# Short tail tiles of a routed expert layer in slots of their own, with float32 products side by side on half the array's columns

## Chip, cores and metric

One core of one Trainium2 chip. The metric is the device time of one execution in microseconds (us), the median over several runs. An array engine (TensorE, "PE") multiplies; VectorE ("DVE"), ScalarE ("ACT") and GpSimd ("POOL") work on tiles; SyncE ("SP") issues most transfers.

## What is computed

Three layers follow one another: a clustered attention (batch 2, 8 heads, 768 positions, head width 64), a gated feed-forward layer, and an expert layer that sends each of 1536 tokens to one of 8 experts. The last is what the change touches:

```python
h = x @ w_in
x = (h * sigmoid(h)) @ w_out                   # (1536, 512) -> (1536, 2048) -> (1536, 512)
logits = x @ w_gate + modality_bias[modality_id]
e_idx = argmax(logits, axis=1)                 # one expert for each token
gate = softmax(logits)[e_idx]
for e in range(8):
    m = e_idx == e
    out[m] = gate[m] * (relu(x[m] @ w1[e]) @ w2[e])     # 512 -> 1024 -> 512
```

For the inputs that are timed the experts get 1, 1, 91, 688, 300, 455, 0 and 0 tokens. All data are float32.

## The kernel before

The kernel goes through attention (about 0 to 260 us of the span), the gated layer (to about 540) and the expert layer. The order of the instructions on every engine is fixed when the program is built: each step is given to a list scheduler by `op(engine, estimated ns, function, deps, uses, alloc, prio)`, with the buffers that it uses, and the scheduler writes one static order per engine. In the code below, numbers in `prio`, `xfer` and after `op("PE", ...` are such planning values.

**Routing.** As the rows of the gated layer's output are finished, they are written to DRAM together with their 8 logits (`x2d`), and DVE works out the expert of each token and its rank within the expert. When the last logits are there, `count()` (L1173) counts the tokens, and from them the number of 128-row tiles of each expert (`nt`, by comparing the counts with 0, 128, 256 and so on) and the first tile of each expert (`cux`). `tiles()` (L1182) makes a one-hot table `bt` from each token's tile; twelve products of `bt` with a matrix of token numbers (L1189) give, for each tile (column) and row (partition), the token's number: `idin`, with a large offset `padb` for rows that stand empty. It also works out each tile's expert (`eti`) and whether that differs from the tile before. The first two tiles belong to the first expert and are known earlier. Experts are taken in a cyclic order that begins with the first full one, here expert 3.

**Tiles.** `slot()` (L1319) is one tile: 128 rows of one expert. `NBASE` = 16 such tiles are always in the program; a conditional block (`rest()`, L1455) holds the others up to 21 and runs only if there are more. The sixteen here are 6, 3, 4, 1, 1 and 1 tiles of the six experts, so that the expert changes in front of tiles 6, 9, 13, 14 and 15 (counted from 0). A tile does this:

- weights: 8 chunks of 512 KB (four of `w1`, four of `w2`), loaded on SP's queue (L1312, L1315) only if the expert has changed, each into one buffer of its own (`w4`), which the tile before must have read;
- split: float32 products in full tiles are made as three products of a shorter format (fp32r): high by high, high by low, low by high. So every tile splits each chunk again, high part by ACT (L202), low part by DVE (L200), into one of ten `whl` buffers;
- gather: POOL fetches the 128 rows by their numbers (L1355); four transposes on PE (L1360) and a split (ACT L1364, DVE L1367) make `xb`;
- first layer (L1381): 8 steps of three products, 128 rows by 512 columns, the sum of 512 inputs in four chunks; ACT takes the positive part (L1396); eight transposes (L1401) and a split (ACT L1406, DVE L1409);
- second layer (L1423): 8 steps of three products; ACT scales by the gate (L1446), POOL scatters the rows to the output (L1449). The scatter's row numbers lie in a small buffer `gt`, of which there are two; DVE writes them (L1435) when the scatter that used the buffer before has landed.

Of the kernel before, what the change touches and what calls it, by code (L numbers as in the profile page):

```python
# [176 lines left out]
F32 = mybir.dt.float32  # L177
F32R = mybir.dt.float32r
# [9 lines left out]
P = 128  # L188
# [570 lines left out]

NT, DM, DF, F2, NE = 1536, 512, 2048, 1024, 8  # L760
NTC = NT // P
NBASE = 16
NFIRST = 2
NSLOT = NTC + NE + 1
XR = DM + NE
X8 = 768

# [4 lines left out]
def moe(tc, sc, pools, att, xT, w_in, w_out, mod_id, w_gate, mod_bias, w1, w2, out, ident, tails, opts):  # L772

    nc = tc.nc
    if True:
# [14 lines left out]
        def op(eng, dur, fn, prio=0.0, **kw):  # L790
            return sc.op(eng, dur, fn, prio=prio + 1000.0, **kw)
# [17 lines left out]
        def main():  # L809
            if a_ops:  # L810
                pools.close("a_ps", "a_sb", "a_cst")
            pools.open("m_sb", reuse_waits="tile")
            pools.open("m_ps", space=PSUM, reuse_waits="tile")
            late.update(Am=pools["m_sb"].tile([P, NTC, P], F16, name="Am"), bt=pools["m_sb"].tile([P, NTC, NSLOT], F16, name="bt"))
# [13 lines left out]
        io1 = small("io1", [P, NSLOT])  # L828
        thr = small("thr", [P, NTC])
        ebg = small("ebg", [P, NE], BF16)  # L830
        wg = small("wg", [P, 4, NE])
        mids = small("mids", [P, 2, NC6, 2], I32)
# [4 lines left out]
        def consts():  # L837
            g = nc.gpsimd
            kw = dict(allow_small_or_imprecise_dtypes=True)
            g.iota(io128, [[1, P]], base=0, channel_multiplier=0, **kw)  # L840
            g.iota(iop, [[0, 1]], base=0, channel_multiplier=1, **kw)
            g.iota(ids, [[S, 2], [1, NC6]], base=1, channel_multiplier=NC6, **kw)
            g.iota(io8, [[1, NE]], base=0, channel_multiplier=0, **kw)
            g.iota(tie8, [[-1, NE]], base=NE, channel_multiplier=0, **kw)
            g.iota(io1, [[1, NSLOT]], base=0, channel_multiplier=0, **kw)
            g.iota(thr, [[P, NTC]], base=0, channel_multiplier=0, **kw)
            g.memset(ones, 1.0)
            g.memset(ebg, 0.0)

        def consts2():  # L850
            V.tensor_scalar(tri, io128, iop[:, 0:1], None, ALU.is_gt)
        o_c = op("Pool", 1800, consts, prio=0)
        o_c2 = op("DVE", 300, consts2, deps=[o_c], prio=50)

# [169 lines left out]
        cmp_, xn = small("cmp_", [P, NE, NTC]), small("xn", [P, NE, NE])  # L1024
        ntot, ntoti = small("ntot", [P, 1]), small("ntoti", [P, 1], I32)
        tt, et = [small(n, [P, NSLOT]) for n in ("tt", "et")]
        dd = small("dd", [P, NSLOT, NE])
        e0i, eti = small("e0i", [P, 1], I32), small("eti", [P, 2, NSLOT], I32)
        idin, padb = small("idin", [P, NSLOT], U32), small("padb", [P, NSLOT])
# [4 lines left out]
        def chain(eng, prio, deps, steps, lat=None, dur=80, uses=()):  # L1034

            o = None
            for n, f in enumerate(steps):
                f, d = f if isinstance(f, tuple) else (f, dur)
                o = op(eng, d, f, deps=(deps if o is None else [o]), uses=uses if n == 0 else (), prio=prio, lat=lat)
            return o  # L1040
# [130 lines left out]
                lambda: V.tensor_scalar(padb[:, :NFIRST], ib.tile[:, :NFIRST], 0.0, 4096.0, ALU.is_equal, ALU.mult)], uses=[ib])  # L1171

        def count(o, lb, pr):  # L1173
            stat["nt"] = chain("DVE", pr + 5, [o, stat["e0"]], [
                lambda: V.tensor_tensor(cnt, lb.tile[:, 2 * NE:3 * NE], gapv, ALU.add),
                lambda: V.tensor_tensor(cmp_, cnt.unsqueeze(2).to_broadcast([P, NE, NTC]),
                                        thr.unsqueeze(1).to_broadcast([P, NE, NTC]), ALU.is_gt),
                lambda: V.tensor_reduce(nt, cmp_, AX.X, ALU.add),
                lambda: V.tensor_tensor(xn, before, nt.unsqueeze(1).to_broadcast([P, NE, NE]), ALU.mult),
                lambda: V.tensor_reduce(cux, xn, AX.X, ALU.add)], uses=[lb])  # L1180

        def tiles(pr):  # L1182

            ib = Buf("bank")

            def f():
                ib.tile = pst(ib)
                for j in range(NTC):
                    nc.tensor.matmul(ib.tile[:, :NSLOT], late["Am"][:, j], late["bt"][:, j], start=(j == 0), stop=(j == NTC - 1))  # L1189
            b12 = lambda v: v.unsqueeze(1).to_broadcast([P, NTC, NE])  # L1190
            o = chain("DVE", pr + 5, [stat["nt"]] + [stat["r", j] for j in range(NTC)], [
                (lambda: V.tensor_tensor(pm, ohb, b12(cux), ALU.mult), 165),
                (lambda: V.tensor_reduce(rk, pm, AX.X, ALU.add), 165),
                lambda: V.tensor_tensor(rk, rk, rkf[:, 0], ALU.add),
                (lambda: V.tensor_tensor(late["bt"], io1.unsqueeze(1).to_broadcast([P, NTC, NSLOT]),
                                         rk.unsqueeze(2).to_broadcast([P, NTC, NSLOT]), ALU.is_equal), 320)])
            o = op("PE", 400, f, deps=[o] + [stat["A", j] for j in range(NTC)], uses=[ib], alloc=[ib], prio=pr)
            stat["i", 1] = chain("DVE", pr + 5, [o], [
                lambda: V.tensor_scalar(idin[:, NFIRST:], ib.tile[:, NFIRST:NSLOT], -1.0, 0.0, ALU.add, ALU.max),
                lambda: V.tensor_scalar(padb[:, NFIRST:], ib.tile[:, NFIRST:NSLOT], 0.0, 4096.0, ALU.is_equal, ALU.mult)], uses=[ib])  # L1200

            stat["e"] = chain("DVE", pr + 5.5, [stat["nt"]], [
                lambda: V.tensor_tensor(cue, cux, nt, ALU.add),
                lambda: V.tensor_reduce(ntot, nt, AX.X, ALU.add),
                lambda: V.tensor_scalar(tt, io1, 1.0, ntot[:, 0:1], ALU.add, ALU.min),
                (lambda: V.tensor_tensor(dd, be(tt), bt8(cue), ALU.is_gt), 230),
                (lambda: V.tensor_reduce(et, dd, AX.X, ALU.add), 230),
                lambda: V.tensor_tensor(eti[:, 1, 1:], et[:, 1:], et[:, :-1], ALU.not_equal),
                lambda: V.tensor_scalar(tt, et, est[:, 0:1], float(NE), ALU.add, ALU.is_ge),
                lambda: V.scalar_tensor_tensor(et, tt, -float(NE), et, ALU.mult, ALU.add),  # L1210
                lambda: V.tensor_scalar(eti[:, 0], et, est[:, 0:1], None, ALU.add),
                lambda: V.tensor_copy(ntoti, ntot)])  # L1212

        cp = dict(w1=-55.8, w2=-29.9, ws=4.5, m1=-25.6, m2=1.6, tx=-46.9, rl=-24.5, ga=-47.5, g0=15, g4=15, gx=14, hi='AAAAAAAA', lo='DDDDDDDD', xyh='DDAAAADD', xyl='DDDDDDDD')
        cp.update(opts.get("C", {}))
        EN = {"A": "Act", "D": "DVE", "P": "Pool"}
        for b in range(2):
# [19 lines left out]
            for fc in range(16):  # L1237
# [4 lines left out]
                for x in range(2):  # L1242
# [76 lines left out]
        def slot(op, t):  # L1319
# [130 lines left out]
                                             bounds_check=NT - 1, oob_is_err=False)  # L1450
            o = op("Act", 570, fo, deps=[o, oe], uses=[ob, os_, eb], alloc=[os_], prio=pr)
            op("Pool", 1040, fs, deps=[o], uses=[os_, eb], prio=pr + 20, xfer=728, name=f"scatter{t}")
        for t in range(NBASE):
            slot(op, t)
        def rest():  # L1455
# [74 lines left out]
```

## Time and profile before

| what | value |
|---|---|
| median of 3 runs (lowest to highest) | 761.03 us (760.16 to 762.56) |
| the profiled execution | 761.42 us |
| its span, granted clock of PE | 759.3 us, 0.989 |
| busy: PE, DVE, ACT, POOL | 736.2, 574.7, 519.4, 272.0 us |
| bytes moved by DMA | 93.27 MB |

The span runs from the first to the last recorded instruction. A row of the timeline merges neighbouring instructions of one line: its start, its length, the engine, the line of the kernel, what is written and read, the shapes and the number of instructions; at the end, in brackets, how long the engine had stood idle and what ended that. The instructions overlap in the pipeline, so that the time one costs is read from the start of it to the start of the next. PE's clock has two levels here, 2.4 GHz (1.00) and 1.2 GHz.

### The profile page before, as it was taken

Reading aid. Unit: us, or ns where it says so; the run is one execution under the profiler, and the core shown is the slowest. Engines: PE = TensorE matmul, PEld = TensorE weight load, DVE = VectorE, ACT = ScalarE, POOL = GpSimd, SP = SyncE. Lnnn points to the kernel's source line nnn. Section 1 sums busy time; section 2 is a strip of 40 time slices with the busy share of each in tenths; the row PEclk is TensorE's granted clock in tenths of the full one; section 3 lists DMA queues with packets and bytes.
Section 4 is the critical chain, followed back from the end, with each engine's and each line's share of the span. In section 5 each row is a group of like instructions: output and inputs, shape, how many; then the busy total and the mean of one; then the engine's idle time right before and its main releaser. Section 6 shows DMA issues by size and latency. Waiting matters only on the chain. (4 is left out here: it accounts for less than half of the span.)

```text
span 759.3 us, 12533 instructions
## 1 busy us (share of the span) xinstructions
PE 736.2 (97%) x4286; PEld 644.4 (85%) x4286; DVE 574.7 (76%) x1034; ACT 519.4 (68%) x951; POOL 272.0 (36%) x304
## 2 busy tenths in 40 slices
PE   8999998999999899999999999999999999999995
PEld 7889887999989799999988989998778887888774
DVE  7978898889889698888477444423978869788972
ACT  7989987998998655554344343323659887898772
POOL 6887765887764100000004000000322424434441
PEclk9999999999999999999999999999999999999998
DMA  8852643522240067665206711000211443515961
GB/s 207 187 131 65 161 116 84 129 70 67 73 133 1 22 236 247 246 234 182 85 16 212 294 63 56 28 0 1 85 30 57 145 161 105 165 51 164 336 212 56
DMA packets 58197, 93.27 MB, mean 123 GB/s; under 512 B 27086, under 2 KB 31950, under 8 KB 58128
## 3 DMA queue, kind: packets, MB, share of 16 engines
q1 hardware_dynamic: 55568, 85.00, 37.0%
q0 software_dynamic: 2560, 7.41, 3.1%
q8 instruction: 36, 0.59, 0.3%
q14 instruction: 33, 0.27, 0.1%
HBM read 101.85 MB, written 15.78 MB: 155 GB/s over the span
## 5 line engine op out<-in xcount | busy, mean ns | idle before, releaser
L200 DVE TENSOR_TENSOR whl<-w,whl 128x1024 fp32r<-128x1024 f32 (+2 forms) x132 | 149.4, 1175 | 2.8 <-ACT whl L202 2.6
L1255 PE MATMUL bank<-whl,whl 128*128 128x384 f32 x768 | 146.9, 340 | 1.8 <-DVE whl L205 1.2
L1255 PEld LDWEIGHTS bank<-whl,whl 128*128 128x128 f32 x768 | 136.8, 190 | 7.7 <-DVE whl L205 1.6
L202 ACT ACTIVATE whl<-w 128x1024 fp32r<-128x1024 f32 (+2 forms) x128 | 128.3, 1038 | 13.6 <-DMA w<-in_moe_w_dram 10.3
L1087 POOL TENSOR_SCALAR row<-L,mx 128x8 f32<-128x8 f32 x12 | 4.7, 394 | 271.1 <-DVE mx L1106 146.6
L1381 PE MATMUL bank<-whl,xb 128*128 128x512 f32 x384 | 97.8, 402 | 2.8 <-DVE whl L200 2.3
L602 DVE TENSOR_REDUCE nm<-big 128x1 f32<-128x768 f32 x96 | 91.0, 951 | 12.0 <-PE big L583 10.7
L1423 PE MATMUL bank<-whl,w 128*128 128x512 f32 x384 | 97.7, 401 | 0.0
L608 ACT ACTIVATE p<-big,nm 128x768 f32<-128x768 f32 x96 | 87.7, 914 | 4.0 <-DVE nm L602 3.7
L1381 PEld LDWEIGHTS bank<-whl,xb 128*128 128x128 f32 x384 | 70.4, 189 | 19.2 <-DVE whl L200 3.4
L1423 PEld LDWEIGHTS bank<-whl,w 128*128 128x128 f32 x384 | 71.3, 190 | 15.0
L622 PE MATMUL t<-ident,p 128*128 128x128 f32 x576 | 81.2, 276 | 2.7 <-ACT yb L714 2.0
L622 PEld LDWEIGHTS t<-ident,p 128*128 128x128 f32 x576 | 67.3, 141 | 12.2 <-issue 2.9
L1449 POOL DMA_INDIRECT out_dram<-row,gt_0i x8 | 29.3, 3661 | 65.6 <-ACT row L1446 50.6
L200 DVE TENSOR_TENSOR whl<-wraw,whl 128x1024 fp32r<-128x1024 f32 x31 | 37.9, 1224 | 15.7 <-ACT whl L202 15.7
L202 ACT ACTIVATE whl<-wraw 128x1024 fp32r<-128x1024 f32 x31 | 32.7, 1057 | 20.5 <-DVE wraw L955 16.3
L656 DVE TENSOR_TENSOR pt_1l<-t,pt_1h 128x384 fp32r<-128x384 f32 x66 | 34.9, 553 | 13.4 <-ACT pt_1h L202 12.6
L1355 POOL DMA_INDIRECT row<-x2d,idin x16 | 34.6, 2165 | 12.9 <-DVE ntoti L1212 5.0
L1270 ACT ACTIVATE g_0s<-bank 128x384 f32<-128x384 f32 x16 | 7.9, 492 | 42.7 <-PE bank L1255 42.7
L700 PE MATMUL t<-pt_0h,vn 128*128 128x384 f32 x96 | 35.1, 366 | 1.0 <-POOL yb L200 0.5
L580 PE MATMUL big<-opn_1K,opn_1QQ 128*128 128x384 f32 x96 | 34.7, 361 | 1.1 <-ACT p L608 1.1
L580 PE MATMUL big<-opn_0K,opn_0QQ 128*128 128x384 f32 x96 | 34.5, 364 | 0.8 <-ACT p L608 0.6
(294 smaller groups left out, 1648.8 us busy)
## 6 DMA issues: line engine op xcount, KB each, us to landing
w<-in_moe_w_dram SPq DMA_DIRECT2D x120, 512.0 KB
w<-in_moe_w_out_dram SPq DMA_DIRECT2D x8, 1024.0 KB
wraw<-wsc SPq DMA_DIRECT2D x16, 512.0 KB
wsc<-wraw SPq DMA_DIRECT2D x15, 512.0 KB
w<-in_moe_w_in_dram SPq DMA_DIRECT2D x7, 1024.0 KB
x2d<-row SPq DMA_DIRECT2D x12, 260.0 KB
rawv<-in_v_dram SPq DMA_DIRECT2D x8, 384.0 KB
rawq<-in_q_dram SPq DMA_DIRECT2D x14, 192.0 KB
```

Source lines behind the costliest of these rows:

```text
L200: (nc.vector if e == "DVE" else nc.gpsimd).tensor_tensor(dst, a, b, op)
L202: nc.scalar.activation(dst, a, AF.Copy, scale=1.0 if scale is None else scale)
L580: nc.tensor.matmul(sb.tile[:, x, :HALF], t["QQ"][:, h, cs], t["K1"][:, h, sl(x)], start=True, stop=False)
L602: nc.vector.tensor_reduce(nb.tile, sb.tile[:, :, :HALF], AX.XY, ALU.max, negate=True)
L608: nc.scalar.activation(pb.tile.rearrange("p (a b) -> p a b", a=2), sb.tile[:, :, :HALF], AF.Exp, bias=nb.tile[:, 0:1], scale=1.0, accum_ou ...
L622: nc.tensor.transpose(tbs[x].tile[:, j * P:(j + 1) * P], pb.tile[:, kc * P:(kc + 1) * P], ident)
L656: nc.vector.tensor_tensor(hs(grp["tile"][1], x), src, hs(grp["tile"][0], x).bitcast(F32), ALU.subtract)
L700: nc.tensor.matmul(yb.tile[:, :HALF], o["vb"].tile[:, h, kc, :], grp["tile"][s][:, kc, :], start=(kc == 0 and s == 0), stop=(kc == NC6 - 1 ...
L1255: nc.tensor.matmul(hb.tile[:, :HALF], w[:, ws, dc, fs], xx[:, s, cs], start=(dc == 0 and n == 0), stop=(dc == 3 and n == 2))
L1355: nc.gpsimd.indirect_dma_start(gb.tile, None, x2d[:, :] if t >= NFIRST else x2d[:S], bass.IndirectOffsetOnAxis(idin[:, t:t + 1], 0))
L1381: nc.tensor.matmul(hbs[x].tile, xs_[:, s, dc], w.tile[:, ws, x * 512:(x + 1) * 512], start=(dc == 0 and n == 0), stop=(dc == 3 and n == 2))
L1423: nc.tensor.matmul(ob.tile, hT.tile[:, s, fc * P:(fc + 1) * P], w.tile[:, ws, i * 512:(i + 1) * 512], start=(fc == 0 and n == 0), stop=(fc ...
```

## The change

The last tile of an expert no longer has to be a full one. `count()` compares the counts with a second row of thresholds as well (64, 192, 320 and so on): an expert whose last tile holds 64 tokens or fewer is marked (`sm`), the first four of these in order get a small slot (`six` is its number), and their last tile is taken out of `nt`. `tiles()` moves the tokens of such tails to one of four further columns of the table, and twelve further products (L1257 after the change) give the small slots' row numbers. `NBASE` falls to 12. The counts here give 5, 2, 4 and 1 full tiles and four small slots with 48, 44, 1 and 1 tokens, so that the expert of full tiles changes three times, in front of tiles 5, 7 and 11, and each small slot loads its expert's 8 chunks without condition.

`small_slot()` puts both halves of the array's columns to use: its up to 64 tokens are the 64 stationary columns of two float32 products, which write to the two halves of the partitions of one bank of the accumulator. In the first layer (L1560) each half makes 512 of the 1024 hidden values, in the second (L1588) 256 of the 512 outputs. Nothing is split. Six of its chunks take the `g` buffers of the gated layer (four of them, so that the last two chunks follow in buffers that first products have read) and two a `wt` buffer. For that the `g` buffers' two halves become one tile, and the row buffers fall from 9 to 7. Slots stand at the full tiles 3, 6, 8 and 10.

```diff
-NBASE = 16
+NBASE = 12
+NSM = 4
+SMALL_AT = (3, 6, 8, 10)
...
+NCOL = NSLOT + NSM
...
-        TAGS = {"wraw": 3, "w64": 2, "wt": 1, "whl": 10, "row": 9, "xb": 2, "g": 4, "bank": 8, "w4": 8, "gt": 2, "lgt": 2}
+        TAGS = {"wraw": 3, "w64": 2, "wt": 1, "whl": 10, "row": 7, "xb": 2, "g": 4, "bank": 8, "w4": 8, "gt": 2, "lgt": 2}
...
+                (lambda: V.tensor_tensor(cmp_, bn(cnt, NTC), thr2.unsqueeze(1).to_broadcast([P, NE, NTC]), ALU.is_gt), 165),
+                (lambda: V.tensor_reduce(nf, cmp_, AX.X, ALU.add), 165),
+                lambda: V.tensor_tensor(sm, nt, nf, ALU.subtract),
+                lambda: V.tensor_tensor(xn, before, b8(sm), ALU.mult),
+                lambda: V.tensor_reduce(six, xn, AX.X, ALU.add),
+                lambda: V.scalar_tensor_tensor(sm, six, float(NSM), sm, ALU.is_lt, ALU.mult),
+                lambda: V.tensor_tensor(nt, nt, sm, ALU.subtract),
...
+                (lambda: V.tensor_tensor(pm, ohb, b12(nt), ALU.mult), 165),
+                (lambda: V.tensor_reduce(rkn, pm, AX.X, ALU.add), 165),
...
+                lambda: V.tensor_tensor(rkn, rkf[:, 0], rkn, ALU.is_ge),
...
+                lambda: V.scalar_tensor_tensor(rk, rkn, float(NCOL), rk, ALU.mult, ALU.add),
...
+        def small_slot(s):
...
+                loads.append(op("SP", 475, f, deps=[ov] + loads[-1:], uses=[rb], alloc=[] if c == 5 else [rb], prio=pr + cs["w"] + c, xfer=1456, name="wl"))
...
+                nc.gpsimd.indirect_dma_start(gb.tile, None, x2d[:, :], bass.IndirectOffsetOnAxis(idin[:, col:col + 1], 0))
...
+                    for x in range(2):
+                        nc.tensor.matmul(hb.tile[H[x]], xb.tile[:, dc * P + 64 * x:dc * P + 64 * x + 64], wt_(dc)[:, 512 * x:512 * x + 512],
+                                         start=(dc == 0), stop=(dc == 3))
...
+                        for y in range(2):
+                            nc.tensor.matmul(ob.tile[H[y], :256], hT.tile[:, j * P + 64 * x:j * P + 64 * x + 64], w[:, 256 * y:256 * y + 256],
+                                             start=(fc == 0), stop=(fc == 7))
...
+                nc.gpsimd.indirect_dma_start(out.rearrange("n (y c) -> (n y) c", y=2), bass.IndirectOffsetOnAxis(idsc[:, s:s + 1], 0), os_.tile, None,
+                                             bounds_check=2 * NT - 1, oob_is_err=False)
```

How the order of instructions moves, at three places. First PE around the products that make the row numbers (L1189 before, L1210 after), in the first two full tiles. Before, they follow the first layer of tile 1 (L1381):

```order
L1381 MATMUL bank_6611<-whl_6369,xb_6537 128x512 x3
L1381 MATMUL bank_6624<-whl_6369,xb_6537 128x512 x3
L1381 MATMUL bank_6611<-whl_6384,xb_6537 128x512 x3
L1381 MATMUL bank_6624<-whl_6384,xb_6537 128x512 x3
L1189 LDWEIGHTS Am
L1189 MATMUL bank_6697<-bt,Am 128x21
```

After, four steps of tile 0's second layer (L1477) and the eight transposes of tile 1's hidden values (L1455) have been drawn in front of them:

```order
L1435 MATMUL bank_6564<-whl_6335,xb_6458 128x512 x3
L1435 MATMUL bank_6575<-whl_6335,xb_6458 128x512 x3
L1477 MATMUL bank_6645<-whl_6355,w_1_6601 128x512 x6
L1455 MATMUL bank_6664<-ident,wraw_6650 128x128 x4
L1455 MATMUL bank_6671<-ident,wraw_6650 128x128 x4
L1477 MATMUL bank_6645<-whl_6371,w_1_6601 128x512 x6
L1210 LDWEIGHTS Am
L1210 MATMUL bank_6698<-bt,Am 128x21
```

Second, PE at the end of the last full tile after the change: the small products (L1560 first layer, L1588 second, `g` and `wt` the buffers of their chunks) of slots 2 and 3 stand between the steps of the second layer of tiles 10 and 11 (L1477). Here the order shows the last first-layer products of slot 3 and the later second-layer products of slot 2, where before there were only full steps:

```order
L1560 MATMUL bank_8398<-g_1w,xb_8258 64x512 x2
L1560 MATMUL bank_8398<-g_3w,xb_8258 64x512 x2
L1560 MATMUL bank_8398<-g_0w,xb_8258 64x512 x2
L1560 MATMUL bank_8398<-g_2w,xb_8258 64x512 x2
L1477 MATMUL bank_8421<-whl_8306,w_1_8401 128x512 x6
L1588 MATMUL bank_8309<-g_1w,w_0_8298 64x256 x4
L1571 MATMUL bank_8443<-ident,wraw_8425 128x128 x4
L1477 MATMUL bank_8421<-whl_8366,w_1_8401 128x512 x6
L1477 MATMUL bank_8421<-whl_8383,w_1_8401 128x512 x3
L1588 MATMUL bank_8309<-g_0w,w_0_8298 64x256 x4
L1477 MATMUL bank_8421<-whl_8383,w_1_8401 128x512 x3
L1477 MATMUL bank_8421<-whl_8392,w_1_8401 128x512 x3
```

So the chunk in `g_1w`, loaded anew after the first of these rows has read the buffer, is used again five rows later, and the one in `g_0w` seven rows after its own. Third, the last entries of SP's queue after the change (L1369 loads a chunk of `w2`; the rows of the address computation between them are left in):

```order
L1369 DMA wt_0a<-in_moe_w_dram 128x2x512
L1369 ISA
L1369 DMA wt_0x<-in_moe_w_dram 128x2x512
L1369 ISA
L1369 DMA g_1w<-in_moe_w_dram 128x2x512
L1369 ISA
L1369 DMA g_3w<-in_moe_w_dram 128x2x512
L1369 ISA
L1369 DMA g_0w<-in_moe_w_dram 128x2x512
L1369 ISA
L1369 DMA g_2w<-in_moe_w_dram 128x2x512
L1620 COMPARE_AND_BRANCH
```

The last two chunks of slots 2 and 3 are the four loads at its end, behind everything else; before, the queue ended with chunks of full tiles.

## Rows read from the trace of the kernel before

**Rows 1.** Busy time, share of the span and instructions of each engine, from the page.
```profile
PE 736.2 (97%) x4286; PEld 644.4 (85%) x4286; DVE 574.7 (76%) x1034; ACT 519.4 (68%) x951; POOL 272.0 (36%) x304
```

**Rows 2.** Stages: stretch, length; busy PE, PEld, DVE, ACT, POOL; clock; DMA share, GB/s.
```profile
626.40:642.50 16.10, 14.30 (x61) 11.19 (x60) 16.10 (x20) 12.15 (x18) 7.23 (x2) 0.89 0.32 95
642.50:655.00 12.50, 12.50 (x62) 10.24 (x61) 9.34 (x13) 11.67 (x17) 4.43 (x2) 1.00 0.36 121
704.60:718.60 14.00, 12.93 (x62) 10.15 (x61) 13.41 (x17) 10.57 (x16) 7.17 (x2) 1.00 0.98 338
```

**Rows 3.** Timeline of PE, tile 8: start, duration, line, operation, count; then idle before.
```profile
642.54 1.55 PE L1381 MATMUL bank<-whl,xb 128*128 128x512 f32 x6
643.94 0.60 PE L1360 MATMUL bank<-ident,row 128*128 128x128 f32 x4
644.29 4.44 PE L1381 MATMUL bank<-whl,xb 128*128 128x512 f32 x18
654.98 1.56 PE L1381 MATMUL bank<-whl,xb 128*128 128x512 f32 x6
```

**Rows 4.** Timeline of PE, last stage: where it waited.
```profile
633.28 2.02 PE L1381 MATMUL bank<-whl,xb 128*128 128x512 f32 x5 [1.80 <-DVE whl L200]
635.09 2.56 PE L1423 MATMUL bank<-whl,w 128*128 128x512 f32 x6
713.26 1.33 PE L1401 MATMUL bank<-ident,wraw 128*128 128x128 f32 x8 [1.05 <-ACT whl L202]
732.30 4.18 PE L1381 MATMUL bank<-whl,xb 128*128 128x512 f32 x17 [0.53 <-DVE xb L1367]
736.96 1.43 PE L1381 MATMUL bank<-whl,xb 128*128 128x512 f32 x5 [0.48 <-DVE whl L200]
```

**Rows 5.** Timeline of DVE at tile 6.
```profile
624.34 0.16 DVE L1435 TENSOR_TENSOR gt_0i<-idin,padb 128x1 uint32<-128x1 uint32 x1 [5.42 <-DMA out_dram<-row,gt_0i]
```

**Rows 6.** Timeline of PE in attention: pairs of 64 columns.
```profile
61.42 0.33 PE L583 MATMUL big<-opn_1KX,opn_1QX 96*128 96x384 f32 x1
61.68 0.32 PE L722 MATMUL t<-ident,sums_1r 128*64 128x128 f32 x1
61.69 0.32 PE L722 MATMUL t<-ident,sums_3r 128*64 128x128 f32 x1
61.84 0.27 PE L722 MATMUL t<-ident,sums_1r 128*64 128x128 f32 x1
62.29 0.27 PE L722 MATMUL t<-ident,sums_3r 128*64 128x128 f32 x1
62.49 0.66 PE L622 MATMUL t<-ident,p 128*128 128x128 f32 x4
```

**Rows 7.** Timeline of PE in attention: products on 32 columns, four abreast.
```profile
50.56 0.85 PE L444 MATMUL t<-full,cT 128*32 128x384 f32 x8
51.34 0.66 PE L622 MATMUL t<-ident,p 128*128 128x128 f32 x4
```

**Rows 8.** Timeline of PE in attention: such a product alone.
```profile
18.11 0.83 PE L444 MATMUL t<-full,cT 128*32 128x384 f32 x2 [0.28 <-DVE full L205]
```

**Rows 9.** Timeline of DVE: the chain ahead of the index products.
```profile
554.66 0.25 DVE L1192 TENSOR_TENSOR pm<-ohb,cux 128x96 f32<-128x96 bf16 x1
555.47 0.41 DVE L1195 TENSOR_TENSOR bt<-io,rk 128x252 f16<-128x252 f32 x1
```

**Rows 10.** Timeline of PE: the index products.
```profile
556.62 0.47 PE L1189 MATMUL bank<-bt,Am 128*128 128x21 f16 x12
```

**Rows 11.** Timeline of SP's queue: two weight loads issued.
```profile
738.07 0.38 SPq L1315 DMA_DIRECT2D w<-in_moe_w_dram  x1
739.21 0.37 SPq L1315 DMA_DIRECT2D w<-in_moe_w_dram  x1
```

**Rows 12.** Timeline of ACT: the splits that waited for these loads.
```profile
741.73 1.06 ACT L202 ACTIVATE whl<-w 128x1024 fp32r<-128x1024 f32 x1 [0.40 <-SPq L1458]
744.55 1.07 ACT L202 ACTIVATE whl<-w 128x1024 fp32r<-128x1024 f32 x1 [1.76 <-SPq L1458]
```

More of the change, by code (lines that the diff above doesn't have):

```diff
@@ L813, in main @@
             pools.open("m_ps", space=PSUM, reuse_waits="tile")
-            late.update(Am=pools["m_sb"].tile([P, NTC, P], F16, name="Am"), bt=pools["m_sb"].tile([P, NTC, NSLOT], F16, name="bt"))
+            late.update(Am=pools["m_sb"].tile([P, NTC, P], F16, name="Am"), bt=pools["m_sb"].tile([P, NTC, NCOL], F16, name="bt"))
         sc.op("-", 0, early, deps=[o for o in a_ops if any(u.tag in EARLY for u in o.uses + o.alloc)],
@@ L827, in moe @@
         io8, tie8 = small("io8", [P, NE]), small("tie8", [P, NE])
-        io1 = small("io1", [P, NSLOT])
+        io1 = small("io1", [P, NCOL])
         thr = small("thr", [P, NTC])
+        thr2 = small("thr2", [P, NTC])
+        half = small("half", [P, 1])
         ebg = small("ebg", [P, NE], BF16)
@@ L851, in consts2 @@
             V.tensor_scalar(tri, io128, iop[:, 0:1], None, ALU.is_gt)
+            V.tensor_scalar(half, iop, 64.0, None, ALU.is_ge)
         o_c = op("Pool", 1800, consts, prio=0)
@@ L1026, in moe @@
         tt, et = [small(n, [P, NSLOT]) for n in ("tt", "et")]
+        nf, sm, six, sme = [small(n, [P, NE]) for n in ("nf", "sm", "six", "sme")]
+        rkn, rkd = small("rkn", [P, NTC]), small("rkd", [P, NTC])
+        sq, esf, esi = small("sq", [P, NSM, NE]), small("esf", [P, NSM]), small("esi", [P, NSM], I32)
+        idsc, padc = small("idsc", [P, NSM], U32), small("padc", [P, NSM])
         dd = small("dd", [P, NSLOT, NE])
         e0i, eti = small("e0i", [P, 1], I32), small("eti", [P, 2, NSLOT], I32)
-        idin, padb = small("idin", [P, NSLOT], U32), small("padb", [P, NSLOT])
+        idin, padb = small("idin", [P, NCOL], U32), small("padb", [P, NCOL])
         x2w, stat = [], {}
@@ L1188, in f @@
                 for j in range(NTC):
-                    nc.tensor.matmul(ib.tile[:, :NSLOT], late["Am"][:, j], late["bt"][:, j], start=(j == 0), stop=(j == NTC - 1))
+                    nc.tensor.matmul(ib.tile[:, :NSLOT], late["Am"][:, j], late["bt"][:, j, :NSLOT], start=(j == 0), stop=(j == NTC - 1))
             b12 = lambda v: v.unsqueeze(1).to_broadcast([P, NTC, NE])
@@ L1212, in tiles, with fsm @@
                 lambda: V.tensor_copy(ntoti, ntot)])
+            stat["es"] = chain("DVE", pr + 5.6, [stat["nt"]], [
+                lambda: V.tensor_tensor(sme, sm, io8, ALU.mult),
+                lambda: V.tensor_tensor(sq, six.unsqueeze(1).to_broadcast([P, NSM, NE]), io1[:, :NSM].unsqueeze(2).to_broadcast([P, NSM, NE]), ALU.is_equal),
+                lambda: V.tensor_tensor(sq, sq, sme.unsqueeze(1).to_broadcast([P, NSM, NE]), ALU.mult),
+                lambda: V.tensor_reduce(esf, sq, AX.X, ALU.add),
+                lambda: V.tensor_copy(esi, esf)])
+            os = chain("DVE", pr + 5.7, [o_rk, stat["e"]], [
+                (lambda: V.tensor_tensor(pm, ohb, b12(six), ALU.mult), 165),
+                (lambda: V.tensor_reduce(rkd, pm, AX.X, ALU.add), 165),
+                lambda: V.tensor_scalar(rkn, rkn, -float(NSLOT + NCOL), float(NSLOT + NCOL), ALU.mult, ALU.add),
+                lambda: V.scalar_tensor_tensor(rkd, rkd, float(NSLOT), rkn, ALU.add, ALU.add),
+                (lambda: V.tensor_tensor(late["bt"][:, :, NSLOT:], io1[:, NSLOT:].unsqueeze(1).to_broadcast([P, NTC, NSM]),
+                                         rkd.unsqueeze(2).to_broadcast([P, NTC, NSM]), ALU.is_equal), 130)])
+            is_ = Buf("bank")
+            def fsm():
+                is_.tile = pst(is_)
+                for j in range(NTC):
+                    nc.tensor.matmul(is_.tile[:, :NSM], late["Am"][:, j], late["bt"][:, j, NSLOT:], start=(j == 0), stop=(j == NTC - 1))
+            lo, hi, sc_ = slice(0, 64), slice(64, 128), slice(NSLOT, NCOL)
+            os = op("PE", 400, fsm, deps=[os], uses=[is_], alloc=[is_], prio=pr + 90)
+            stat["i", 2] = chain("DVE", pr + 5.7, [os], [
+                *[lambda r=r: V.tensor_scalar(idin[r, sc_], is_.tile[lo, :NSM], -1.0, 0.0, ALU.add, ALU.max) for r in (lo, hi)],
+                *[lambda r=r: V.tensor_scalar(padc[r], is_.tile[lo, :NSM], 0.0, 8192.0, ALU.is_equal, ALU.mult) for r in (lo, hi)],
+                lambda: V.tensor_scalar(padc, padc, half[:, 0:1], None, ALU.add),
+                lambda: V.scalar_tensor_tensor(idsc, idin[:, sc_], 2.0, padc, ALU.mult, ALU.add)], uses=[is_])
         cp = dict(w1=-55.8, w2=-29.9, ws=4.5, m1=-25.6, m2=1.6, tx=-46.9, rl=-24.5, ga=-47.5, g0=15, g4=15, gx=14, hi='AAAAAAAA', lo='DDDDDDDD', xyh='DDAAAADD', xyl='DDDDDDDD')
@@ L1268, in sig @@
                     def sig(hb=hb, gb=gb):
-                        gb.tile = dict(s=sbt(gb, [P, HALF], F32, "s"), h=sbt(gb, [P, HALF], F32R, "h"), l=sbt(gb, [P, HALF], F32R, "l"))
+                        hl = sbt(gb, [P, 2, HALF], F32R, "w")
+                        gb.tile = dict(s=sbt(gb, [P, HALF], F32, "s"), h=hl[:, 0], l=hl[:, 1])
                         nc.scalar.activation(gb.tile["s"][:, :HALF], hb.tile[:, :HALF], AF.Sigmoid)
@@ L1453, in moe @@
+        cs = dict(pr=14.0, w=-48.0, ga=-45.0, tx=-40.0, m1=-12.0, rl=-11.0, m2=0.0)
         for t in range(NBASE):
             slot(op, t)
+            for s in range(NSM):
+                if SMALL_AT[s] == t:
+                    small_slot(s)
         def rest():
```

104 lines of the change are left out of this document (93 added, 11 removed).

## The prediction

> **What bounds the kernel now.** The profiled execution took 761.42 us, 0.39 above the median of the runs shown (761.03); its span is 759.3. I read the busy totals first [rows 1]: TensorE is busy for 97% of the span, every other engine for less. Then the stage that the change touches, cut by tile [rows 2]: in an undisturbed tile (642.5 to 655.0) PE is busy for the whole 12.5 us at full clock, DVE for 9.3 and ACT for 11.7. So in this stage a TensorE microsecond saved is a microsecond of span, unless the split of weights (ACT copy, DVE subtract) or a transfer then ends last. The instructions of such a tile in order of time [rows 3] give its price: one tile begins at 642.54, the next at 654.98: **12.44**. Six products take 1.40 (642.54 to 643.94), one 0.234; four transposes add 0.35.
>
> Three tiles are longer, and [rows 4] show where: tile 7 loses 3.7 us (PE waits 1.80 for a split, and the products behind run at half clock, six in 2.56 where 1.55 is usual [rows 3, 4]; the stage view grants 0.89 for that tile [rows 2]), tile 13, 14.0 long [rows 2], loses 1.5 behind a wait of 1.05, and the last tile 1.3 (waits of 0.53 and 0.48, and a little behind them). In all **6.5 us**. Behind the largest stands an order of DVE: at 624.34 it has waited 5.42 us, with splits queued behind, for the landing of a scatter whose index buffer it must overwrite [rows 5].
>
> **The change part by part.** The inputs' tokens per expert, in the order used, make 6, 3, 4, 1, 1, 1 tiles. The last tiles of four experts hold 48, 44, 1 and 1 tokens, which is 64 or fewer; so exactly 12 full tiles (5, 2, 4, 1) and 4 small slots run, and the conditional block does not.
>
> *Removed:* four tiles, 4 x 12.44 = **49.8 us**.
>
> *Small products.* A float32 product passes through the array twice. A slot has four pairs over 512 columns, 8 passes, and for the second layer eight pairs over 256, 16 passes. Rows that show such a pair stand in attention [rows 6]: 64 stationary columns each, starts 0.01 apart (61.68 and 61.69), the next pass 0.16 later, and from 61.84 four more until 62.28, 0.11 each, for 128 moving columns (the last one's twin is the row of 62.29). So 0.44 a pass of 512 and 0.22 of 256: 8 x 0.44 + 16 x 0.22 = 7.04 a slot. The ends: 2.4 GHz at two clocks a column makes 6.83; the products of 384 columns on quarter arrays, four abreast, made two passes in 0.78 (50.56 to 51.34 [rows 7]), 0.34 each when 0.10 for leaving (next step) is taken off: 7.25 a slot. I take 7.04, the nearest form. Two sets of four transposes add 2 x 0.35. Sum 7.74, four slots **31.0** (30.1 to 31.8).
>
> *Switching.* Between a full-array product and half columns the pace breaks [rows 6]: 61.42 to 61.68 is 0.26 for 384 columns that at 2.4 GHz take 0.16, the first pass is 0.05 longer, and leaving (62.29 to 62.49) takes 0.20, 0.10 more than a pass. That is 0.25 a group, and the order shows 16 groups: **4.0**.
>
> *Routing.* Twelve dependent DVE operations join the chain in front of the index products. The last links of the chain of before follow one another in 0.27 (three from 554.66 to 555.47 [rows 9]), so the tile list is 12 x 0.27 = 3.2 us later. The order covers it: four second-layer steps and eight transposes, 12 x 0.234 + 2 x 0.35 = 3.5 us of TensorE, now stand ahead of the index products. If that cover fails, the loss is at most the 3.2. Twelve extra small index products cost about what the twelve of before take: 0.47 [rows 10], **0.5**. The later DVE operations for the small slots have more than a tile before anybody needs them: nothing.
>
> TensorE: -49.8 + 31.0 + 4.0 + 0.5 = **-14.3**.
>
> *ACT and DVE.* Four tiles' splits go; a slot brings four ACT operations and two tiny DVE ones. Per tile of PE time both engines gain slack: nothing to pay.
>
> *Stalls.* Before, five changes of expert lost 6.5, 1.3 each. Now there are three: 3.9. New are four unconditional loads of eight 512 KB chunks. Seven sets and the rows make 37 MB in 190 us, 200 GB/s on average where 338 were moved in a tile [rows 2]; bandwidth is no bound, lateness is. In every slot the last two chunks go into buffers that the products of a first layer (for slot 2, those of slot 3) must have read. Between release and use the order puts, with the prices above, 6.7 and 6.8 us of products in slot 0, 6.9 and 7.2 in slot 1, 4.0 and 5.6 in slot 2. Issued at 738.07, a chunk released ACT at 741.73, 3.7 later; the one issued at 739.21 released it 2.8 after that [rows 11, 12]. When the queues are full a chunk passes in 1.55 (524 KB at 338 GB/s [rows 2]). The first chunk of a group is then in time everywhere (3.7 against 4.0 at least). The last stands third or fourth in its queue: with 1.55 for each ahead of it nothing is late; with 2.8 slot 0 loses 0.4, slot 1 2.3, slot 2 1.9, together 4.6. I take the middle, **2.3**. Stalls after: 6.2 instead of 6.5, **-0.3** (none: -6.5; the dear end 8.5: +2.0).
>
> *Tail.* The last tile's scatter follows its last product as before, with two half-row scatters queued on POOL in front, which the order places some 5 us of products earlier: nothing.
>
> Sum: 761.42 - 14.3 - 0.3 = 746.8, by the median 0.4 less, 746.4: **746 us**. Ends: 740 without any stall and 739 with the cheap products as well; 749 with the dear transfers, 750 with the dear products too.
>
> **The rivals.**
> 1. *All stalls go*: fewer splits give DVE enough slack that neither the scatter wait nor the small loads reach TensorE: **740**. For it: DVE's load falls. Against it: in this order the last three full tiles share one index buffer, so the same wait for a scatter stands there still.
> 2. *Pairs overlap in part.* The rows show a pair as cheap as one, but there both halves move the same tile; here each half has its own 512 columns. If a quarter of the second product's time is added, the 28.2 us of products become 35.3: +7.1, **754**. The four products abreast speak against it: eight records, four products, took 0.85, and one product alone 0.83 [rows 7, 8]. The Trainium skill ("TensorE: Matmul & The Clock Gate", section "Measured speedup vs the span model") lists a gain of 2.38 for three column tiles of 512 columns, 0.79 a tile; a pair would then gain 1.59 and the products take 35.5, an estimate that comes to the same 754. No row here shows a pair on 512 columns; the pairs on 128, at 0.11, took what 2.4 GHz gives one pass alone.
> 3. *No overlap at all* with two moving tiles: a pair takes both times, +28.2: **775**, slower. It decides from the point where 60% of the second product's time is added (16.9 of 28.2 us). Against it stand the starts 0.01 apart.
> 4. *Small loads come late*: a slot's chunks queue behind the eight of a full tile (8 x 1.55 = 12.4). A chunk then lands 12.4 + 3.7 after release where some 6 us of products stand: 10 a slot, 746 - 2.3 + 40 = **784**, slower. It decides from 4.2 us a slot beyond the forecast. For it: one queue (SP) issues all, and tiles 13 and 14 had it 98% busy [rows 2]. Against it: those were three changes in a row; now a slot stands between.
> 5. *Not what it says*: more than 12 tiles would run the conditional block of nine, over 100 us more; the counts exclude it but for an error in the new arithmetic.
>
> **How the numbers follow.** What a measurement of this kernel can tell from no change is 0.3%, 2.3 us: faster is below 758.7, slower above 763.3. Forecast 0.73 (0.01 of it within), rival 1 0.08, rival 2 0.07, rival 4 0.07 (0.02 within, 0.05 slower), rival 3 0.04, rival 5 0.01. Faster 0.72 + 0.08 + 0.07 = 0.87; same 0.03; slower 0.05 + 0.04 + 0.01 = 0.10. Range **739 to 755**: from no stalls and cheap products to rival 2 with a part of the dear transfers.
>
> **What would show it.** Right: passes of pairs 0.44 apart on 512 columns and 0.22 on 256; idle time in front of them by their chunk's DMA of a few us in all, mostly in slots 1 and 2; about 12.44 for each full tile less what is woven in; granted clock near 1 but for one or two tiles. Wrong: passes of 0.88 (rival 3) or about 0.55 (rival 2); waits for small chunks above 4 us in each slot (rival 4); DVE or ACT ending most waits of TensorE, which would make the split the bound.

## The result and the profile after

The changed kernel takes **749.25 us** (median of 4 runs, 748.30 to 752.37) against 760.88 for the kernel before in the same comparison: ratio 0.9851, 95% interval 0.9818 to 0.9884. 746 was forecast with a range of 739 to 755, so the time lies inside it; of the 15 us of gain that were forecast, 11.6 came.

The profiled execution took 749.2 us with a span of 747.4. Its busy totals, which answer to [rows 1]:

```profile
PE 721.6 (97%) x4282; PEld 617.4 (83%) x4282; DVE 537.3 (72%) x1014; ACT 483.9 (65%) x911; POOL 235.1 (31%) x305
```

PE lost 14.6 us of work, DVE 37, ACT 36, and PE still bounds the span. The next two rows are the last stage as one stretch each, from the first product of tile 0 to the end of the last product, after and then before (columns as in [rows 2]):

```profile
541.10:736.20 195.10, 191.48 (x1015) 140.08 (x1011) 136.62 (x271) 130.03 (x202) 42.10 (x38) 0.99 0.56 192
```

```profile
540.70:750.40 209.70, 205.57 (x1019) 165.46 (x1015) 174.12 (x290) 164.77 (x242) 79.34 (x37) 0.99 0.42 139
```

The stage fell from 209.7 to 195.1 us, **14.6 less**, and the forecast for it was 14.3 + 0.3. But from the last product to the end of the span there were 9.0 us before (750.35 to 759.3) and 11.2 after (736.16 to 747.4). The end took back **2.3 us**, and the stage began 0.4 later (among the executions of this study it begins anywhere from 539.9 to 543.1).

The small slots in PE's timeline: a first layer of slot 1, and three chunks of its second layer.

```profile
654.68 1.08 PE L1560 MATMUL bank<-g_0w,xb 128*64 128x512 f32 x4
655.59 1.03 PE L1560 MATMUL bank<-g_2w,xb 128*64 128x512 f32 x4
657.31 1.03 PE L1560 MATMUL bank<-g_3w,xb 128*64 128x512 f32 x4
658.27 0.66 PE L1543 MATMUL bank<-ident,row 128*128 128x128 f32 x4
...
661.12 1.08 PE L1588 MATMUL bank<-wt_0a,w 128*64 128x256 f32 x8
662.04 1.03 PE L1588 MATMUL bank<-wt_0x,w 128*64 128x256 f32 x8
663.86 2.37 PE L1435 MATMUL bank<-whl,xb 128*128 128x512 f32 x9
```

A row is one chunk: two passes of a pair of 512 columns, or four of 256. The starts lie 0.91 apart at the entry (654.68, 655.59) and 0.86 after it (655.59 to 657.31 is two chunks), so 0.43 a pass; leaving takes 0.96. A whole first layer, 654.68 to 658.27, is 3.59; with 0.10 for leaving taken off, two such layers are 7.0 us a slot, where 7.04 was forecast from passes of 128 columns [rows 6].

The stalls that are left, in the same view:

```profile
602.37 0.66 PE L1455 MATMUL bank<-ident,wraw 128*128 128x128 f32 x4 [1.03 <-ACT wraw L1450]
...
625.19 0.97 PE L1455 MATMUL bank<-ident,wraw 128*128 128x128 f32 x4 [2.37 <-ACT wraw L1450]
625.81 3.70 PE L1477 MATMUL bank<-whl,w 128*128 128x512 f32 x9
629.35 0.60 PE L1543 MATMUL bank<-ident,row 128*128 128x128 f32 x4
```

Two waits, 1.03 and 2.37, both before the transposes of hidden values, both for ACT's part that cuts the products off at zero (L1450); after the second one nine products take 3.54 us (625.81 to 629.35, granted clock 0.58) where 2.11 is usual. In all 4.8 us, against 6.5 before and 6.2 in the forecast. No product waited for the DMA of a small chunk in this execution. What ACT did before the two waits, with its own idle time in brackets:

```profile
594.38 1.06 ACT L202 ACTIVATE whl<-w 128x1024 fp32r<-128x1024 f32 x1 [1.51 <-DMA w<-in_moe_w_dram]
597.12 1.06 ACT L202 ACTIVATE whl<-w 128x1024 fp32r<-128x1024 f32 x1 [1.68 <-DMA w<-in_moe_w_dram]
...
601.73 0.59 ACT L1450 ACTIVATE wraw<-bank 128x512 f32<-128x512 f32 x1
...
618.53 0.58 ACT L1450 ACTIVATE wraw<-bank 128x512 f32<-128x512 f32 x1
622.16 2.00 ACT L202 ACTIVATE whl<-w 128x1024 fp32r<-128x1024 f32 x2 [3.05 <-PE bank L1477]
...
624.53 0.60 ACT L1450 ACTIVATE wraw<-bank 128x512 f32<-128x512 f32 x1
```

ACT stood at the splits of tile 5's new weights for 1.51 and 1.68 us, waiting for their DMA, and everything behind them in its fixed order came later, the cut at 601.73 too. The second time the first half of the cut ran at 618.53, the second half only at 624.53: two splits stand between them in ACT's order, and they could not start before 622.16. The row puts their wait of 3.05 down to a product (L1477). In the second execution of the same kernel (below) the same two splits, at the same place of ACT's order, waited for a load of weights:

```profile
622.00 2.01 ACT L202 ACTIVATE whl<-w 128x1024 fp32r<-128x1024 f32 x2 [2.22 <-DMA w<-in_moe_w_dram]
```

So a load is the likely cause in the first execution too. The stretch ahead of it, 609 to 622, with busy times, clock, DMA share and GB/s as in [rows 2]:

```profile
609.00:622.00 13.00, 12.89 (x78) 9.09 (x77) 8.63 (x13) 6.54 (x12) 2.97 (x3) 1.00 1.01 370
```

The DMA engines were busy the whole time there, at 370 GB/s.

The routing chain and the index products, DVE then PE:

```profile
556.94 0.25 DVE L1213 TENSOR_TENSOR pm<-ohb,cux 128x96 f32<-128x96 bf16 x1
559.29 0.42 DVE L1221 TENSOR_TENSOR bt<-io,rk 128x252 f16<-128x252 f32 x1
```

```profile
560.33 0.46 PE L1210 MATMUL bank<-bt,Am 128*128 128x21 f16 x12
562.81 0.46 PE L1257 MATMUL bank<-bt,Am 128*128 128x4 f16 x12
```

The table `bt` is ready 3.8 us later than before (559.29 against 555.47 [rows 9]), 3.4 when the later start of the stage is taken off, with 3.2 forecast; PE took up the index products without waiting, so the cover held.

Last the end. PE's last products, among them the last ones of slot 2 (`g_0w`) and slot 3 (`g_2w`); POOL's scatters, with idle time and what ended it, in brackets; the last scaling on ACT; then two pieces of the chain that ended last, which is the work followed back from the last instruction.

```profile
729.00 1.08 PE L1588 MATMUL bank<-g_0w,w 128*64 128x256 f32 x8
734.24 1.03 PE L1588 MATMUL bank<-g_2w,w 128*64 128x256 f32 x8
735.20 0.96 PE L1477 MATMUL bank<-whl,w 128*128 128x512 f32 x3
```

```profile
730.88 0.98 POOL L1607 DMA_INDIRECT out_dram<-row,idsc  x1 [8.31 <-ACT row L1604]
736.07 0.98 POOL L1607 DMA_INDIRECT out_dram<-row,idsc  x1 [4.20 <-ACT row L1604]
739.89 0.98 POOL L1503 DMA_INDIRECT out_dram<-row,gt_1i  x1 [2.84 <-ACTq L1620]
```

```profile
736.20 0.69 ACT L1500 ACTIVATE row<-bank,gt_1s 128x512 f32<-128x512 f32 x1 [0.41 <-PE bank L1477]
```

```profile
736.07 2.97 DMA out_dram<-row,idsc
...
740.19 0.68 POOL out_dram L1503
```

The last full tile's rows were scaled by 736.89 (736.20 + 0.69). Their scatter started at 739.89, because POOL first waited until the scatter of small slot 3, launched at 736.07, had landed 2.97 us later. POOL's own row names ACT's queue at a branch (L1620) for this wait; the chain names the landing, and the run without that scatter (below) decides for the landing. Before, the last two scatters lay 4.9 us apart, and the last one followed its scaling (750.38 to 751.07) by 0.3:

```profile
750.38 0.69 ACT L1446 ACTIVATE row<-bank,gt_1s 128x512 f32<-128x512 f32 x1 [4.20 <-PE bank L1423]
746.46 1.27 POOL L1449 DMA_INDIRECT out_dram<-row,gt_0i  x1 [12.14 <-ACT row L1446]
751.35 0.98 POOL L1449 DMA_INDIRECT out_dram<-row,gt_1i  x1 [3.62 <-ACT row L1446]
```

### The profile page after: what moved, and what is told of

Its sections match the earlier page's. It is cut to its first block, busy times and chain, and to the rows that moved or that the text cites. A ratio compares the mean times of both kernels' runs of the same rounds, so it can differ in the third digit from the quotient of the medians.

```text
span 747.4 us, 12406 instructions
## 1 busy us (share of the span) xinstructions
PE 721.6 (97%) x4282; PEld 617.4 (83%) x4282; DVE 537.3 (72%) x1014; ACT 483.9 (65%) x911; POOL 235.1 (31%) x305
## 5 line engine op out<-in xcount | busy, mean ns | idle before, releaser
L200 DVE TENSOR_TENSOR whl<-w,whl 128x1024 fp32r<-128x1024 f32 (+2 forms) x100 | 113.4, 1166 | 24.4 <-ACT whl L202 24.0
L202 ACT ACTIVATE whl<-w 128x1024 fp32r<-128x1024 f32 (+2 forms) x96 | 95.9, 1029 | 20.6 <-PE bank L1435 12.6
L602 DVE TENSOR_REDUCE nm<-big 128x1 f32<-128x768 f32 x96 | 91.1, 952 | 11.6 <-PE big L583 10.2
L1435 PE MATMUL bank<-whl,xb 128*128 128x512 f32 x288 | 74.9, 404 | 0.0
L1477 PE MATMUL bank<-whl,w 128*128 128x512 f32 x288 | 74.8, 404 | 0.0
L1477 PEld LDWEIGHTS bank<-whl,w 128*128 128x128 f32 x288 | 53.5, 192 | 13.0 <-issue 1.6
L1435 PEld LDWEIGHTS bank<-whl,xb 128*128 128x128 f32 x288 | 51.9, 188 | 14.5 <-issue 3.1
L1349 PE MATMUL bank<-whl,g_0w 128*128 128x512 f32 x144 | 38.5, 394 | 0.0
L1349 PE MATMUL bank<-whl,g_1w 128*128 128x512 f32 x144 | 37.6, 394 | 0.0
L1349 PE MATMUL bank<-whl,g_2w 128*128 128x512 f32 x144 | 37.4, 394 | 0.0
L1349 PE MATMUL bank<-whl,g_3w 128*128 128x512 f32 x144 | 36.7, 395 | 0.0
```

What stands on the lines that cost most here:

```text
L200: (nc.vector if e == "DVE" else nc.gpsimd).tensor_tensor(dst, a, b, op)
L202: nc.scalar.activation(dst, a, AF.Copy, scale=1.0 if scale is None else scale)
L602: nc.vector.tensor_reduce(nb.tile, sb.tile[:, :, :HALF], AX.XY, ALU.max, negate=True)
L1349: nc.tensor.matmul(ab.tile, gb.tile[gs][:, js], w[:, ws, fc % 2], start=(fc == 0 and n == 0), stop=(fc == 15 and n == 2))
L1435: nc.tensor.matmul(hbs[x].tile, xs_[:, s, dc], w.tile[:, ws, x * 512:(x + 1) * 512], start=(dc == 0 and n == 0), stop=(dc == 3 and n == 2))
L1477: nc.tensor.matmul(ob.tile, hT.tile[:, s, fc * P:(fc + 1) * P], w.tile[:, ws, i * 512:(i + 1) * 512], start=(fc == 0 and n == 0), stop=(fc ...
```

## The experiments

Three questions were put: are the terms of the sum what they seem, is the longer end the wait on POOL, and what causes the two stalls. The kernel before varies more on the later chips (753.6 to 763.6), so the profiled executions, cut at the same places, are compared beside the medians. The changed kernel was run again beside three of the runs only (749.30 there, 749.25 the first time); the others are set against these two times.

**Everything but the small slots.**

```diff
-NBASE = 12
+NBASE = 16
...
-                lambda: V.scalar_tensor_tensor(sm, six, float(NSM), sm, ALU.is_lt, ALU.mult),
+                lambda: V.scalar_tensor_tensor(sm, six, 0.0, sm, ALU.is_lt, ALU.mult),
...
-            for s in range(NSM):
-                if SMALL_AT[s] == t:
-                    small_slot(s)
```

> Sixteen full tiles and no small slots, but all of the change's routing, its 7 row buffers and its joined g tile. If the gain lies in tiles alone, this stands with the kernel before plus the 12 small index products: 761.4 (760.5 to 762.5). If the longer routing chain is not covered, up to 764; if buffers gave a part of the gain, below 759.

761.71 us against 758.29 of the kernel before, ratio 1.0036 (1.0008 to 1.0064). Routing, buffers and the joined tile bring no gain; they cost 0.6 to 4.9 us by the interval, with 0.5 expected. In the trace the stage is not longer than before (208.4 against 209.7); this execution began it 2.4 later. Where the cost lies is open.

**Twelve full tiles alone.** The last part of the edit above, nothing else.

> Twelve full tiles, small slots left out (the 94 tokens of the four short tails get no output). Four tiles at 12.44 are 49.8 below the sixteen: 711 if the slots cost TensorE 36 us and the end 2.3 as the trace reads. If the slots' loads also cause the two stalls of the changed kernel (about 5 us), 706.

707.82 us, between the two forecasts: the stalls of the slots are gone, but the twelve tiles alone have 2.4 us of idle time on PE. The stage of the sixteen tiles and that of the twelve:

```profile
543.10:751.50 208.40, 204.10 (x1031) 164.90 (x1027) 177.35 (x319) 164.35 (x241) 70.88 (x38) 1.00 0.42 140
```

```profile
542.40:698.50 156.10, 153.74 (x791) 124.17 (x787) 133.03 (x263) 119.07 (x177) 51.86 (x30) 1.00 0.37 124
```

52.3 us for four tiles; PE's idle time in the stage was 4.3 and 2.4 (length less busy time), so 50.4 of work, where 49.8 was forecast. The changed kernel's stage is 39.0 above the twelve tiles (195.1 less 156.1); with idle time and half-clock products taken off both (3.6 and 1.4; 2.4), four slots cost 36.4 us of PE, where 31.0 + 4.0 had been forecast. The end is 8.7 without small slots (698.5 to 707.2).

**No pairs.** Both products of a pair go to one half of the columns, one after the other; the second layer makes 512 columns in one product of 64 rows.

```diff
-                        nc.tensor.matmul(hb.tile[H[x]], xb.tile[:, dc * P + 64 * x:dc * P + 64 * x + 64], wt_(dc)[:, 512 * x:512 * x + 512],
+                        nc.tensor.matmul((hb, hb1)[x].tile[H[0]], xb.tile[:, dc * P + 64 * x:dc * P + 64 * x + 64], wt_(dc)[:, 512 * x:512 * x + 512],
...
-                        for y in range(2):
-                            nc.tensor.matmul(ob.tile[H[y], :256], hT.tile[:, j * P + 64 * x:j * P + 64 * x + 64], w[:, 256 * y:256 * y + 256],
+                        nc.tensor.matmul(ob.tile[H[0]], hT.tile[:, j * P + 64 * x:j * P + 64 * x + 64], w,
...
```

> The same small slots with both products of a pair on the same half of the columns, one after the other, and one product of 512 columns in the second layer. If pairs run at the price of one, each slot loses what pairing saved, 7.0 us, 28 in all, and the kernel is slower than before: 777. If pairs only overlapped in part, the loss is smaller, 20 or less.

772.62 us, ratio 1.0173 (1.0112 to 1.0234) to the kernel before: slower than the sixteen tiles. A chunk of slot 1 now takes 1.72, start to start, where the pair takes 0.86:

```profile
659.82 1.88 PE L1560 MATMUL bank<-g_2w,xb 128*64 128x512 f32 x4
661.54 1.88 PE L1560 MATMUL bank<-g_1w,xb 128*64 128x512 f32 x4
```

32 chunks at 0.86 more are 27.5 us; the stage grew by 22.5 (217.3 against 194.8 in the unaltered kernel beside it), because with more PE time in between nearly all stalls went (0.3 us of waits instead of 4.5). So pairs run at the price of one, and the whole gain rests on them.

**Without the last small scatter.**

```diff
-            op("Pool", 1040, fs, deps=[o], uses=[os_], prio=pr + 20, xfer=364, name=f"scatters{s}")
+            if s != 3:
+                op("Pool", 1040, fs, deps=[o], uses=[os_], prio=pr + 20, xfer=364, name=f"scatters{s}")
```

> The changed kernel without the scatter of the last small slot (its one token gets no output); order of the engines else as it was. If the last scatter of full rows waits on POOL for that one's landing, the span ends 2.3 to 2.7 us earlier: 746.7. If the longer end has another cause (the branch, the ACT that scales), 749.

745.79 us, 3.5 below the changed kernel, which was not run beside it. Against the kernel before, which was, the ratio is 0.9852 and the change's own 0.9851, so the times alone do not decide. The trace does: the end is 8.6 (733.1 to 741.7), 2.6 less, and POOL's last scatter starts 0.3 after its rows are scaled:

```profile
727.77 0.98 POOL L1607 DMA_INDIRECT out_dram<-row,idsc  x1 [8.31 <-ACT row L1604]
734.06 0.98 POOL L1503 DMA_INDIRECT out_dram<-row,gt_1i  x1 [5.31 <-ACT row L1500]
```

This execution, the fastest of the four (743.60), also has a stage 2.8 shorter, with less waiting at the same two places (0.6 and 1.4). The longer end is that wait.

**The last small slot earlier**, at full tile 9, by `SMALL_AT = (3, 6, 8, 9)`.

> The last small slot stands at full tile 9 instead of 10, so that its scatter lands long before the last full tile's. If the end is longer only because the last scatter waits on POOL for the small one's landing, the end after the last product falls from 11.2 to about 8.8 and the time by 2.4; if bunching two slots at 8 and 9 makes their chunks late, products wait by DMA for small chunks, 2 us or more, and it is even or slower.

749.53 us: even. The end is 8.5, 2.7 less than after, but products now wait for small chunks, which stand in PE's waits (waiter, what it waited for, us in total, times, longest):

```profile
PE bank L1588 <- DMA wt_0x<-in_moe_w_dram: 1.2, 1, 1.2
PE bank L1588 <- DMA g_1w<-in_moe_w_dram: 0.9, 1, 0.9
PE bank L1588 <- DMA g_3w<-in_moe_w_dram: 0.4, 1, 0.4
```

2.5 us of them; what the end gave, the second slot in a row of two took back. Both halves of the expectation came.

**The changed kernel again**, as a base for the three runs beside it.

> The changed kernel unaltered, as a base on the same chip for the three beside it: 746 to 750, both stalls before the hidden transposes again in the same places, 2 to 5 us in all.

749.30 us, its end 11.1. Its waits on PE:

```profile
PE bank L1455 <- ACT wraw L1450: 2.7, 2, 1.5
PE bank L1588 <- DMA wt_0x<-in_moe_w_dram: 1.1, 1, 1.1
PE bank L1588 <- DMA g_0w<-in_moe_w_dram: 0.7, 1, 0.7
```

The same kernel here waits 1.8 us for small chunks of slot 2, and 2.7 at the two old places: the single execution above, with none for small chunks, was one draw of several. The forecast's 2.3 is of the right size.

**Thin loads**, an eighth of the small slots' bytes.

```diff
-                    wsrc(c, ev["e"], dst)
+                    thin(c, ev["e"], dst)
...
+            four = lambda v, n, m: v[:, :m].unsqueeze(1).to_broadcast([P, n, m])
```

Here `thin` loads 128 columns of a chunk of `w1`, 2 x 64 of one of `w2`, and the products read them through `four`, repeatedly.

> The small slots' chunks are loaded to an eighth and the products read that eighth eight times (wrong values for 94 tokens), same count and shape of instructions. If the slots' 16.8 MB make the full tiles' weights late and so cause the two stalls before hidden transposes (1.0 and 2.4 us, with 1.6 at half clock), about 744. If the stalls come from ACT's fixed order, 749.

743.90 us (742.61 to 745.88). PE's waits in the stage are down to one:

```profile
PE bank L1455 <- ACT wraw L1450: 0.8, 1, 0.8
```

The stage is 190.3 us instead of 195.1 with the same instructions; the end stays at 11.1. So the bytes of the slots' loads cost nearly all of the stalls, though for the most part not at the small products: they make the full tiles' weights late, ACT waits at their split, and the cut that stands behind in its order is late for PE. The stretch that answers to 609 to 622 above:

```profile
606.00:618.00 12.00, 12.00 (x74) 8.50 (x73) 8.81 (x13) 6.78 (x14) 2.59 (x3) 1.00 0.80 246
```

The number of loads and their order on SP's queue are the same in this run, so it is not their place in the queue alone that costs; the DMA engines' share falls from 1.01 to 0.80.

**A plan that knows the loads.** The planner is told of weight transfers at tiles 0, 5, 7, 11 instead of every third tile.

```diff
-                           prio=pw + c - 5 if t else 150 + c, xfer=1456 if t % 3 == 0 or t > 12 else 0, name="wl")
+                           prio=pw + c - 5 if t else 150 + c, xfer=1456 if t in (0, 5, 7, 11) else 0, name="wl")
```

> The planner is told of the weight loads where they really come with these inputs (tiles 5, 7, 11 instead of every third); nothing else. If the two stalls come from a fixed order that expects those weights earlier than the shared queue brings them, an order that knows gains 3 to 5 us; if the queue itself is the limit there, nothing changes by more than 1.

748.74 us (746.12 to 750.32), 0.6 below the base and inside its scatter: inconclusive alone. In the profiled execution, the fastest of the four (746.12), the stage is 1.5 shorter (193.3); waits for small chunks (1.9 us) and a few short ones stand where the two long ones stood.

**Both together.** The last slot is drawn forward by a part of a tile only (4 or 8 units of priority of the 20 that make a tile), without and with that plan.

```diff
-            pr = 300.0 + 20 * tp + cs["pr"]
+            pr = 300.0 + 20 * tp + cs["pr"] - (8 if s == 3 else 0)
```

> The last small slot planned by 4 units of priority sooner (20 make a tile): its four second-layer chunks then stand together, with 18 full products (4.2 us) behind them, so its scatter should land before the last full one's is due. If the longer end is that wait alone, 2.4 us go, less nothing: 746.9. If its chunks then come late (3.7 us for one alone), 2 us come back at the small products and it is even, 749.

> The same by 8 units: both late slots drawn apart, 24 full products behind the last small one, two groups of half-column products fewer (0.25 each). End 2.4 shorter, switching 0.5 less: 746.4; if the small chunks are late as in the run at tile 9 (2.5 us there), 749.

> Four units sooner and the planner told of the real weight loads (tiles 5, 7, 11). If the two gains add, 2.4 at the end and 1.5 in the products: 745.4; if the stalls only change place, 747.

> Eight units sooner and the planner told of the real loads. Both gains and the switching: 744.9; if the stalls only change place, 747.

Measured: 747.02, 746.73, 745.61 and **743.92** us (743.48 to 745.76), where 746.9, 746.4, 745.4 and 744.9 were expected if the gains come; the last with a ratio of 0.9793 (0.9760 to 0.9825) to the kernel before. The ends are 8.5 to 8.8 in all four. In the first two, products wait 3.2 and 2.6 us for small chunks, and their stages (195.7 and 194.8) are no shorter than that of the base (194.8), so that the times fell by 2.3 and 2.6 only through the end; with the plan the waits shrink too (stages of 194.0 and 192.4). The last one's waits on PE and its last scatters:

```profile
PE bank L1477 <- DVE whl L200: 0.9, 1, 0.9
PE bank L1588 <- DMA g_2w<-in_moe_w_dram: 0.7, 2, 0.4
PE bank L1588 <- DMA wt_0a<-in_moe_w_dram: 0.6, 1, 0.6
```

```profile
729.42 0.98 POOL L1607 DMA_INDIRECT out_dram<-row,idsc  x1 [2.56 <-ACT gt_1e L1486]
734.66 0.98 POOL L1503 DMA_INDIRECT out_dram<-row,gt_1i  x1 [4.26 <-ACT row L1500]
```

The small scatter starts 5.2 us before the last one, which follows its own scaling without a wait for the landing. This version beats both kernels; every one of its runs is below every run of the changed kernel, which was not run beside it. Its plan is written for these inputs' expert changes.

## Why the prediction was right, and where it was off

The stage fell by 14.6 us, to the tenth what was forecast, and that is partly luck: the removed tiles gave 0.6 more, the slots cost 1.4 more and the stalls 1.4 less than their terms.

- *Removed tiles* (49.8 forecast): 50.4 by the two runs without small slots.
- *Small products* (31.0): passes of 0.43 and 0.215 against 0.44 and 0.22. The form seen in attention, on 128 columns with one moving tile for both halves, carried over to 512 and two moving tiles. Rival 3 fell by the trace, and rival 2 too: a pair gained 2.0 (1.72 against 0.86). The estimate of 1.59 from the Trainium skill's 2.38 for three column tiles ("TensorE: Matmul & The Clock Gate", section "Measured speedup vs the span model") was too low for pairs of this form, where the measurement decides; three tiles, the form of that figure, were not run. Rival 5 fell as well: the full tiles have 288 first-layer products, 24 a tile, which makes twelve.
- *Switching* (4.0): the entry shows 0.05 in the first chunk, leaving 0.10. Slots with their switches cost 36.4 by difference, 35.0 forecast. With the passes measured, products and transposes make 30.3 of it, which leaves 6.1 for the 16 groups, 0.38 each instead of 0.25: an estimate by difference, which holds whatever else a slot costs PE.
- *Routing* (0.5): covered. The chain grew by 3.4 instead of 3.2; PE never waited for it, and the new index products take 0.31 (562.81 to 563.12).
- *Stalls* (-0.3, from 6.5 to 6.2): 4.8 in the profiled execution, 4.5 of waits in the second one. The sum held, its working only in part. The 6.5 before are not 1.3 for each change of expert, since 3.7 of them stood behind a scatter's landing [rows 5]. The forecast looked for lateness in the slots' own last chunks: none and 1.8 us in two executions of the changed kernel, 1.3 to 3.2 in the last four orders. It left out that the same bytes delay the full tiles' weights, which the thin loads showed to be the larger part here; "bandwidth is no bound" came from an average (192 GB/s over the stage), while the DMA engines were fully busy from 609 to 622. One of the forecast's own signs of being wrong was seen: ACT ended all of PE's waits. They are 3.4 us in all and go with the bytes, so the split has not become the bound. Rival 1 (all stalls go) and rival 4 (4 us a slot) both fell.
- *Tail* ("nothing"): **this step failed.** Both small scatters were placed "some 5 us of products earlier" than the last one. That holds for slot 2, whose last product ends 6.2 us before the last full one (730.01, 736.16), but not for slot 3: behind its last chunk the order has only three full products, 1.0 us (735.20 to 736.16). And the forecast did not ask whether the next scatter may start before that one lands. The two last scatters start 3.8 us apart where the products that they follow end 1.0 apart, and the end grew by 2.3; with 5.2 us between them, in the last version above, it did not grow. That is most of the 3 us between forecast and result; with the end mended, the kernel stands at 746.7 to 747.0.

## What to carry to other kernels

Where a tile is mostly empty, two float32 products side by side on the two halves of the columns do with a quarter less of PE's time (36.4 us for four slots, 50.4 for four tiles), and without the pairing the same rearrangement loses. After a change of order, read the end of the program by itself: writes to one tensor that wait for each other's landing cost most of a landing (2.3 us of 2.97 here) if the last two come close together. Added loads are paid, here for the larger part, where another engine's fixed order waits for other loads, not only where their own data are used; an average of the bandwidth does not show it.

## What was not expected of the hardware

- Scatters of this kernel to the output start one after the other's landing: 2.97 us from launch to landing, 0.85 more until the next starts. POOL's queue holds semaphore waits of the scatter's line (L1503) right ahead of it, at 739.1; whether the chip would demand the wait without them wasn't tried.
- Two float32 products of 64 stationary columns with different moving tiles of 512 columns take 0.86 us together, on one half of the columns 1.72.
- The same program on the same inputs shows its waits in different places from execution to execution (small chunks 0 and 1.8 us, the cut 3.4 and 2.7), while the two executions took 749.2 and 749.4 us.
